# Two PSUM evacuations that may run on ScalarE or VectorE, in an attention and feed-forward kernel whose order a scheduler writes

## The chip, the cores and the metric

The kernel runs on one core of a Trainium2 chip. The metric is the device time of one execution, in microseconds, as the median of several runs. A profiled execution gives the trace from which the rows below are read. Engines are named as in the profile: PE is the matrix engine (PEld its weight loads), ACT is ScalarE, DVE is VectorE, POOL is GpSimd, SP issues most of the DMAs (SPq in the trace).

## The reference, cut to what matters

```python
# S = 2048 rows, D = 448, H = 16 heads of 28, N = 4 segments of 512 rows, F = 1792
g = sigmoid((x * gate_w).sum(-1, keepdims=True))
for s in range(4):                                   # a: attention with a memory
    p = softmax(qs @ ks.T * scale + mask)            # inside the segment
    o = gb * (phi(qs) @ M / (phi(qs) @ z + 1e-6)) + (1 - gb) * (p @ vs)
    M, z = M + phi(ks).T @ vs, z + phi(ks).sum()
a = concat(o) @ wo
b = silu(x @ w1) @ w2                                # the feed-forward
out = g * a + (1 - g) * b
```

## The kernel before

Matrix operands are split into a high and a low half in 16 bits, and a product is the sum of three products of halves. The program is one stream per engine. Nobody writes that stream by hand: every step is handed to `Sched` as a task with its engine, a cost, the steps it depends on, the buffers it takes and a priority, and `Sched.run` picks the next task of each engine by earliest possible start and then by priority. A task may name two engines; `start_of` then lets an engine have it only if it would not end later there than on the other engine by more than `slack`. The constants at the head of the file (priorities, offsets, prices) are the table that shapes this order.

The stages in the order of time:

- Loads, splitting, and the projections q, k, v for all four segments (up to about 163 us in the trace before). The memory part of the attention runs here too (L1052, L1054, L1089, L1090).
- The change of stage (about 146 to 185 us): the first feed-forward products (L632 on `wa`, the first weight matrix, with the short last pieces of two products at L1238 and L1239), the maxima of the scores for the first heads (PE L737, then DVE L744 to L750) and the first softmax heads all start here.
- The attention of the 64 pairs of head and segment, between which feed-forward products are placed (185 to 458 us). One head is a chain: four score matmuls (PE L1355) into three PSUM tiles `sc`; three exponentials (ACT L1360) into `pf`; two causal masks (POOL L1363, L1366); the high half (ACT L1372); the low half in three pieces (POOL L1376); twenty short matmuls with v (PE L1389); one sum (DVE L1397).
- The second half of the feed-forward and the output product (L632 on `wos`), with the result leaving by DVE L1466 and L1470 (458 us to the end).

A feed-forward unit has the steps of `after` in `unit`: e1 is a tanh from PSUM (ACT L1211), e2 multiplies in PSUM (DVE L1213), e3 writes the high half of g to SBUF (ACT L1215), e4 writes the low half (DVE L1217) and frees the PSUM tile. The products with the second weight matrix (PE L1259) read both halves. In the first of the two feed-forward passes each partial sum of 128 rows leaves PSUM by `part` (ACT L1298) for a scratch tensor in HBM.

PSUM has eight tiles: three `sc` (scores, maxima, later the output product), one `cc` for the short attention matmuls, and four (`mm` and a `cc` tile given over at the change of stage) for the feed-forward. Weights pass through two staging tiles `rawf` in turn: SP loads one, ACT L606 writes the high half, DVE L595 or POOL L597 and L598 the low half, and then the staging tile can be loaded again. The rows of q and k of a group of four heads come to SBUF in the tile `ring` by four DMAs, and the maxima of that group (PE L737) wait for all four. SP is one queue: a DMA that waits for a buffer holds back what stands behind it.

Of the kernel before, what the change touches and what calls it, by code (L numbers as in the profile page):

```python
# [13 lines left out]
AF = mybir.ActivationFunctionType  # L14
OP = mybir.AluOpType
# [3 lines left out]
S, D, H, DH, NSEG, L, F = 2048, 448, 16, 28, 4, 512, 1792  # L19
# [8 lines left out]
SCALE = DH ** -0.5  # L28
LIFT = 8.0 * math.log(2.0)
TALL = 2.0 ** 15  # L30
TWINP = 165.57
TWO = 0.33
NEG = -1.0e30
NT = NSEG * NG
# [12 lines left out]
DOWN = 2.0 ** -19  # L47
TINY = 2.0 ** -40
FIT = 2.0 ** -15
WOT = 154.32  # L50
TUS = 1.6
TLAT = 4.0
SLACK = -0.5
LOP = 35.82
LATE = -0.07
FIRST = 165.32
WPRIO = 28.79
MAXO = 63.55
FULL = 0.111
LOCK = 0.06  # L60
RB = "cc"
# [2 lines left out]
VA = 12.33  # L64
VS = 0.91
NV = 8
XH0 = -75.6
NF = 4
VE = 6.18
LASTQ = 6.73  # L70
WQS = -122.17
VH = 29.33
XS0 = -34.76
VC = -7.5
OT1 = -143.04
XS = 35.55
QS = -29.35
KS1 = -24.75
SS = -14.29

# [3 lines left out]


PRICE = 267.48
PRICE2 = 150.04
SLACK2 = 0.15
PVRUNS = [((1, 0), 1)]
PVP = 86.58  # L90
FLO = 41.44
FHI = 709.77
WOP = 85.61
SZ = 13.48
SZSTEP = 0.12
XPRIO = 324.18
WBP = 27.13
XLEAD = 146.82


# [180 lines left out]
def infini_mix(ctx: ExitStack, tc: tile.TileContext, x, wq, wk, wv, wo, beta, w1, w2, out):  # L281
    nc = tc.nc
    out = out.rearrange("b s d -> (b s) d")
    ctx.enter_context(tc.manual_schedule())
    sch = Sched()
# [47 lines left out]
    def act(cols, fn, *deps, **k):  # L333
        return sch.add("ACT", 0.06 + 0.00083 * cols, fn, deps, **k)
# [13 lines left out]
    def either(cols, fn, *deps, **k):  # L348
        eng = {"DVE": nc.vector, "POOL": nc.gpsimd}
        return sch.add(("DVE", "POOL"), (0.07 + 0.00104 * cols, 0.1 + 0.00224 * cols), lambda e: fn(eng[e]), deps, port=True, **k)  # L350

    def scaled(cols, fn, *deps, **k):
        eng = {"DVE": nc.vector, "POOL": nc.gpsimd}
# [27 lines left out]
    cols, at = {}, 0  # L381
# [17 lines left out]
    ogs = const.tile([128, NSEG * TB], F32, name="ogs")  # L399
# [787 lines left out]
    BK["cc"].give(BK["mm"])  # L1187
    sch.price, sch.slack = PRICE2, SLACK2

# [16 lines left out]
    def unit(s, fs, prio, finish, gate=(), tail=False):  # L1206
        gt = {}
        t1, t2 = {}, {}
        def after(f, ps, g, m, p0):
            th = Buf(TH)  # L1210
            e1 = sact(L, lambda ps=ps, th=th: nc.scalar.activation(th.v, ps.v, AF.Tanh, scale=ths[:, s:s + 1]), m, takes=[th],  # L1211
                     uses=[ps], prio=p0)
            e2 = dve(L, lambda ps=ps, th=th: nc.vector.scalar_tensor_tensor(  # L1213
                ps.v, th.v, 1.0, ps.v, op0=OP.add, op1=OP.mult), e1, uses=[ps, th], prio=p0)
            e3 = act(L, lambda ps=ps, g=g: nc.scalar.activation(g.v[:, 0], ps.v, AF.Copy, scale=DOWN), e2,  # L1215
                     uses=[ps, g], prio=p0)
            e4 = dve(L, lambda ps=ps, g=g: nc.vector.scalar_tensor_tensor(  # L1217
                g.v[:, 1], ps.v, DOWN, g.v[:, 0], op0=OP.mult, op1=OP.subtract), e3, uses=[ps, g], prio=p0)
            gt[f] = g, [e3, e4]
            t1[f] = m  # L1220

        own = [f for f in fs if f != FREE]
        for a, b in zip(own[::2], own[1::2] + [None]):
            held = []
            for f in (a, b):
                if f is None:
                    continue
                p0 = prio(11 * L if b is None else 10.5 * L)
                ps, g = Buf(BK["mm"]), Buf(GTR)
                w, wd = WA[f]  # L1230
# [4 lines left out]
            if b is not None:  # L1235
                def both(held=held):
# [4 lines left out]
                       prio=held[1][4])  # L1241
# [5 lines left out]
        for tb in range(TB):  # L1247
            ps = Buf(BK["mm"])
            p0 = prio(3 * len(fs) * D)
            sl = slice(tb * 128, (tb + 1) * 128)  # L1250
            last, lasts = None, []
            halves = [(0, 3 * D // 4), (3 * D // 4, D)] if tail and tb == TB - 1 else [(0, D)]
            for lo, hi in halves:
                for j, f in enumerate(fs):
                    g, w = gt[f][0], WB[f][0]

                    def go(g=g, w=w, j=j, ps=ps, sl=sl, lo=lo, hi=hi):
                        for i, (y, z) in enumerate(((0, 0), (0, 1), (1, 0))):
# [3 lines left out]
                              takes=[ps] if last is None else [],  # L1262
                              uses=[ps, g, w], prio=p0)
# [31 lines left out]
    def part(s, tb, ps, lasts, prio):  # L1295
        k = s * TB + tb
        a = Buf(PA)
        w = act(D + 110, lambda: nc.scalar.activation(a.v, ps.v[:, :D], AF.Copy, scale=ogs[:, k:k + 1]),  # L1298
                lasts[-1][0], takes=[a], uses=[ps], prio=prio)
        PST[k] = dma(229e3, lambda: start(pscr[s][tb * 128:(tb + 1) * 128, :], a.v), w, uses=[a], prio=prio)  # L1300

    def weights(fs, t1, t2, prio):
# [115 lines left out]
    prio = spread(FLO, FHI, NSEG * len(PASSES[0]) * (11 * L + TB * 3 * D))  # L1418
# [126 lines left out]
```

## Time and profile before

| | |
|---|---|
| median of 3 runs | 550.6 us (549.58 to 551.15) |
| the profiled execution | 550.8 us |
| its span, first to last instruction | 549.0 us |
| mean granted clock of PE | 0.997 |
| PE busy | 538.8 us, 98% of the span |
| DVE, ACT, POOL busy | 74%, 74%, 64% |

The execution is 1.8 us longer than its span. Busy time of PE is the time covered by records of matmuls; a record is longer than the time at which the next one may follow, so short gaps do not show as idle time.

### The profile page before, as it was taken

What the parts mean: (1) busy time and instruction counts of PE and PEld (TensorE: products, weight loads), DVE (VectorE), ACT (ScalarE), POOL (GpSimd) and SP (SyncE); (2) the same over time, 40 slices, a digit from 0 to 9 for tenths busy, and PEclk for the clock granted to TensorE, in tenths of its full rate; (3) what the DMA queues carried; (4) which work ended last, traced back from release to release, by engine and by line L of the source; (5) the groups of instructions that cost most, each with busy time, mean ns of one, the idle gap of its engine ahead of it and who ended that gap; (6) DMA issues with size and microseconds to landing.
All of it is one profiled execution on the core that took longest, in us unless ns stands there. A gap on an engine that the chain in (4) does not pass through costs nothing.

```text
span 549.0 us, 11601 instructions
## 1 busy us (share of the span) xinstructions
PE 538.8 (98%) x4028; PEld 295.7 (54%) x4028; DVE 408.9 (74%) x1005; ACT 406.3 (74%) x696; POOL 354.0 (64%) x552
## 2 busy tenths in 40 slices
PE   9999999999998999999999999999999999999997
PEld 3445656565543565555656555565555554555544
DVE  5999899999758785688756789767897219764473
ACT  5979988765357988799887999789997897601140
POOL 3135476834506779889899989998998997211220
PEclk9999999999998999999999999999999999999999
DMA  8778876635475334233333334454311211789962
GB/s 299 251 235 271 239 231 179 207 97 142 145 194 156 102 87 137 72 84 84 90 86 103 87 89 123 119 154 128 83 38 54 87 51 43 265 210 243 258 167 79
DMA packets 78378, 79.19 MB, mean 144 GB/s; under 512 B 44232, under 2 KB 68040, under 8 KB 78320
## 3 DMA queue, kind: packets, MB, share of 16 engines
q1 hardware_dynamic: 77744, 77.47, 48.9%
q10 hardware_dynamic: 576, 0.99, 0.6%
q8 instruction: 31, 0.51, 0.4%
q14 instruction: 27, 0.22, 0.1%
HBM read 48.41 MB, written 26.09 MB: 136 GB/s over the span
## 4 chain that ended last, share of the span: by engine, by line
PE 72%; ACT 8%; DMA 6%; DVE 6%; POOL 4%; issue 2%; SPq 1%; DVEq 0%; POOLq 0%; ACTq 0%
PE mm L632 18%; PE mm L1259 17%; PE sc L632 10%; PE cc L1259 6%; PE sc L737 5%; PE sc L1355 5%; PE cc L1389 5%; PE cc L632 3%; ACT pf L1360 3%; DMA rawf<-in_w_dram 2%; POOL phl L1376 2%; ACT phl L1372 1%; DMA k_scr<-stg 1%; DMA xraw<-in_x_dram 1%; PE cc L1089 1%
## 5 line engine op out<-in xcount | busy, mean ns | idle before, releaser
L1376 POOL TENSOR_TENSOR phl<-pf,phl 128x384 f16<-128x384 f32 (+1 forms) x192 | 189.5, 1004 | 24.2 <-ACT phl L1372 24.0
L1360 ACT ACTIVATE pf<-sc,lift,es 128x512 f32<-128x512 f32 (+1 forms) x192 | 127.0, 707 | 18.1 <-PE sc L1355 13.4
L750 DVE CUSTOM_DVE_ANT_0 sc<-sc,mk 128x384 f32<-128x384 f32 (+1 forms) x192 | 104.7, 575 | 26.9 <-PE sc L737 25.0
L1259 PE MATMUL mm<-wb,ghl 128*128 128x448 f16 (+2 forms) x516 | 111.9, 348 | 0.1
L632 PE MATMUL mm<-xh,wa 128*128 128x512 f16 x393 | 101.4, 379 | 0.0
L1259 PEld LDWEIGHTS <-ghl 128*128 128x128 f16 x684 | 64.0, 97 | 52.8 <-issue 1.0
L1372 ACT ACTIVATE phl<-pf 128x1280 f16<-128x1280 f32 x64 | 81.3, 1270 | 9.8 <-POOL pf L1366 9.3
L632 PEld LDWEIGHTS <-wa 128*128 128x128 f16 x524 | 49.1, 98 | 51.7 <-issue 5.2
L1355 PE MATMUL sc<-ring 86*128 86x512 f16 (+3 forms) x256 | 63.6, 301 | 1.4 <-DVE mx L750 1.0
L737 PE MATMUL sc<-ring 84*128 84x128 f16 (+3 forms) x256 | 57.2, 300 | 1.6 <-DVE mx L745 0.7
L1389 PEld LDWEIGHTS <-phl 128*128 128x128 f16 x1280 | 41.9, 96 | 9.1 <-issue 0.6
L1397 DVE TENSOR_REDUCE oraw<-cc 128x116 f32<-128x232 f32 x64 | 25.3, 396 | 27.7 <-PE cc L1389 27.1
L643 POOL TENSOR_TENSOR ol<-ol,ml 128x448 f32<-128x448 f32 x12 | 13.6, 1132 | 49.7 <-DMA ol<-o_scr 39.2
L1389 PE MATMUL cc<-vg,phl 128*128 128x29 f16 (+1 forms) x1280 | 43.8, 182 | 0.3 <-POOL phl L1376 0.2
L632 PE MATMUL mm<-xh,wqs 128*128 128x512 f16 x176 | 43.4, 379 | 0.2 <-DVE vt L1022 0.2
L632 PE MATMUL mm<-xh,wks 128*128 128x512 f16 x176 | 42.1, 380 | 0.0
L649 ACT ACTIVATE oh<-ol,os 128x448 f16<-128x448 f32 x16 | 10.6, 664 | 41.3 <-POOL ol L643 41.2
L1259 PE MATMUL cc<-wb,ghl 128*128 128x448 f16 x168 | 38.7, 352 | 0.0
L1355 PEld LDWEIGHTS <-ring 86*128 86x128 f16 x256 | 24.0, 98 | 24.5 <-issue 4.5
L632 PE MATMUL cc<-xh,wa 128*128 128x512 f16 x131 | 34.9, 390 | 0.9 <-DVE ghl L1217 0.9
L632 PE MATMUL sc<-wos,oT 128*128 128x448 f16 x176 | 35.4, 352 | 0.0
L1366 POOL TENSOR_SCALAR_AFFINE_SELECT pf<-pf 128x384 f32<-128x384 f32 x64 | 33.6, 526 | 2.2 <-ACT pf L1360 1.7
(197 smaller groups left out, 958.1 us busy)
## 6 DMA issues: line engine op xcount, KB each, us to landing
rawf<-in_w_dram SPq DMA_DIRECT2D x26, 256.0 KB
rawf<-in_w_dram SPq DMA_DIRECT2D x28, 224.0 KB
v_scr<-vt SPq DMA_DIRECT2D x16, 232.0 KB
vg<-v_scr SPq DMA_DIRECT2D x16, 232.0 KB
xraw<-in_x_dram SPq DMA_DIRECT2D x14, 256.0 KB
q_scr<-stg SPq DMA_DIRECT2D x16, 224.0 KB
ring<-q_scr SPq DMA_DIRECT2D x16, 224.0 KB
k_scr<-stg SPq DMA_DIRECT2D x16, 224.0 KB
```

The costliest lines, as they stand in the source:

```text
L632: nc.tensor.matmul(ps(), *p[i], start=(i == 0), stop=(i == n - 1 and not more))
L643: d = pool(530, lambda: nc.gpsimd.tensor_add(b.v, b.v, m.v), d, e, uses=[b, m], **k)
L737: nc.tensor.matmul(ps.v[:, u:u + n], rg.v[:KS, 0, hh, i * 128:(i + 1) * 128], rg.v[:KS, 1, hh, :n], start=i + t > 0, stop=(i + t > 0 or j ...
L750: nc.vector.tensor_tensor_reduce(r, r, MK[:, L - n:], 1.0, NEG, OP.add, OP.max, mx.v[:, hh, i:i + 1])
L1259: nc.tensor.matmul(ps.v[:, lo:hi], g.v[:, y, sl], w.v[:, z, lo:hi], start=(j == 0 and i == 0), stop=(j == len(fs) - 1 and i == 2))
L1355: nc.tensor.matmul(ps.v[:, e:e + w], rg.v[:KK, 1, hh, j * 128:(j + 1) * 128], rg.v[:KK, 0, hh, j * 128:], start=True, stop=True)
L1360: ex.append(sact(e, lambda b=b, ps=ps, pf=pf, e=e: nc.scalar.activation(pf.v[:, b, :e], ps.v[:, :e], AF.Exp, bias=lift, scale=es[:, s:s + ...
L1366: mk.append(pool(204, lambda pf=pf: nc.gpsimd.affine_select(pf.v[:, :, :128], pf.v[:, :, :128], [[0, 3], [1, 128]], OP.is_ge, 0.0, base=0, ...
L1372: hi = copy(1280, lambda hl=hl, flat=flat: nc.scalar.activation(hl.v[:, 0], flat(), AF.Copy), *mk, takes=[hl], uses=[pf], prio=p0 + 2)
L1376: low = pool(w - u + 22, lambda hl=hl, flat=flat, u=u, w=w: nc.gpsimd.tensor_sub(hl.v[:, 1, u:w], flat()[:, u:w], hl.v[:, 0, u:w]), low, u ...
L1389: nc.tensor.matmul(p[:, i, :2 - z], hl.v[:, z, u:u + 128], vg.v[:, j, hh, :2 - z], start=(z == zs[0] and i == 0), stop=(z == zs[-1] and j ...
L1397: nc.vector.tensor_reduce(orw.v[:, hh], p, axis=AX.X, op=OP.add)
```

## The change

`out_of` is a new helper: a copy out of PSUM with a scale, as a task that names ACT and DVE. Step e3 of a feed-forward unit and the copy in `part` use it in place of `act`; `Sched` thus gives each of these 68 copies to the engine that it thinks ends it first. Sixteen constants of the table have other values, so the order is written anew.

```diff
+    def out_of(cols, fn, *deps, **k):
+        how = {"ACT": lambda o, i, s: nc.scalar.activation(o, i, AF.Copy, scale=s),
+               "DVE": lambda o, i, s: nc.vector.tensor_scalar(o, i, s, None, op0=OP.mult)}
+        return sch.add(("ACT", "DVE"), (0.06 + 0.00083 * cols, 0.07 + 0.00104 * cols), lambda e: fn(how[e]), deps, **k)
...
-            e3 = act(L, lambda ps=ps, g=g: nc.scalar.activation(g.v[:, 0], ps.v, AF.Copy, scale=DOWN), e2,
-                     uses=[ps, g], prio=p0)
+            e3 = out_of(L, lambda e, ps=ps, g=g: e(g.v[:, 0], ps.v, DOWN), e2, uses=[ps, g], prio=p0)
...
-        w = act(D + 110, lambda: nc.scalar.activation(a.v, ps.v[:, :D], AF.Copy, scale=ogs[:, k:k + 1]),
-                lasts[-1][0], takes=[a], uses=[ps], prio=prio)
+        w = out_of(D + 110, lambda e: e(a.v, ps.v[:, :D], ogs[:, k:k + 1]), lasts[-1][0], takes=[a], uses=[ps], prio=prio)
...
-WOT = 154.32
+WOT = 103.91
...
-LATE = -0.07
+LATE = -0.17
...
-SLACK2 = 0.15
+SLACK2 = -0.35
```

In the program as built, 15 of the 52 copies of g's high half and 6 of the 16 partial sums stand on DVE (L354 of the changed kernel), the others on ACT (L353). The number of PE instructions of each kind is the same. Up to the first maxima of scores (about 106 us in the trace before) PE's rows are the same, and after that they differ in place only. In the changed kernel line numbers from L351 on are 3 to 5 higher: L1217 is L1221 there, L750 is L755, L1215 is L353, L595 is L600, L606 is L611, L1360 is L1363 and L1372 is L1375.

Three places show how rows moved, all at the change of stage.

On DVE, around the low half (L1217) of the third pair of units, whose PSUM tiles are `cc_2216` and an `mm` tile; `L750` pairs are maxima of scores, `wb` is a piece of the second weight matrix. Before, and then now:

```order
L750 ISA sc_2358,mx<-sc_2358,mk 128x512
L750 ISA mx 128x1
L750 ISA sc_2365,mx<-sc_2365,mk 128x384
L750 ISA mx 128x1
L595 SCALAR_TENSOR_TENSOR wb<-rawf,up,wb 128x448
L1217 SCALAR_TENSOR_TENSOR ghl<-cc_2216,ghl 128x512
L1217 SCALAR_TENSOR_TENSOR ghl<-mm_2243,ghl 128x512
```

```order
L755 ISA sc_2359,mx<-sc_2359,mk 128x512
L755 ISA mx 128x1
L1221 SCALAR_TENSOR_TENSOR ghl<-cc_2216,ghl 128x512
L755 ISA sc_2367,mx<-sc_2367,mk 128x384
L755 ISA mx 128x1
L600 SCALAR_TENSOR_TENSOR wb<-rawf,up,wb 128x448 x2
L1221 SCALAR_TENSOR_TENSOR ghl<-mm_2244,ghl 128x512
```

The low half that frees the `cc` tile now stands ahead of one pair of maxima and of the weight piece; the one that frees the `mm` tile now stands behind two weight pieces instead of one.

On SP, the loads of the third `ring` tile (`ring_2133`), between loads of the staging tiles. Before, and then now:

```order
L366 DMA rawf<-in_w_dram 128x448
L366 DMA ring_2133<-q_scr 56x2048
L366 DMA rawf<-in_w_dram 128x448
L366 DMA vg<-v_scr 128x4x232
L366 DMA ring_2133<-q_scr 28x2048
L366 DMA ring_2133<-k_scr 56x2048
L366 DMA rawf<-in_w_dram 128x448
L366 DMA ring_2133<-k_scr 28x2048
```

```order
L371 DMA rawf<-in_w_dram 128x448 x2
L371 DMA ring_2133<-q_scr 56x2048
L371 DMA vg<-v_scr 128x4x232
L371 DMA ring_2133<-q_scr 28x2048
L371 DMA ring_2133<-k_scr 56x2048
L371 DMA rawf<-in_w_dram 128x448 x2
L371 DMA ring_2133<-k_scr 28x2048
```

The last of the four loads of the ring tile now stands behind two staging loads where it stood behind one; each of the two waits for its own staging tile.

On ACT, around the first exponentials and the high half of the first head (`phl`). Before, and then now:

```order
L1360 ACTIVATE pf<-sc_2342,lift,es 128x512
L1360 ACTIVATE pf<-sc_2346,lift,es 128x256
L606 ACTIVATE wb<-rawf,up 128x448
L1215 ACTIVATE ghl<-cc_2216 128x512
L1215 ACTIVATE ghl<-mm_2243 128x512
L1372 ACTIVATE phl<-pf 128x1280
```

```order
L1363 ACTIVATE pf<-sc_2342,lift,es 128x512
L611 ACTIVATE wb<-rawf,up 128x448
L1363 ACTIVATE pf<-sc_2352,lift,es 128x256
L353 ACTIVATE ghl<-cc_2216 128x512
L353 ACTIVATE ghl<-mm_2244 128x512
L611 ACTIVATE wb<-rawf,up 128x448
L1375 ACTIVATE phl<-pf 128x1280
```

A second weight piece now stands between the two high halves of g and the high half of the first head; these two copies of g stay on ACT.

More of the change, by code (lines that the diff above doesn't have):

```diff
@@ L30 @@
 TALL = 2.0 ** 15
-TWINP = 165.57
+TWINP = 125.24
 TWO = 0.33
@@ L53 @@
 SLACK = -0.5
-LOP = 35.82
-LATE = -0.07
-FIRST = 165.32
+LOP = 26.69
+LATE = -0.17
+FIRST = 167.33
 WPRIO = 28.79
-MAXO = 63.55
+MAXO = 63.47
 FULL = 0.111
@@ L66 @@
 NV = 8
-XH0 = -75.6
+XH0 = -75.5
 NF = 4
@@ L70 @@
 LASTQ = 6.73
-WQS = -122.17
+WQS = -125.76
 VH = 29.33
@@ L76 @@
 XS = 35.55
-QS = -29.35
+QS = -29.51
 KS1 = -24.75
@@ L86 @@
 PRICE = 267.48
-PRICE2 = 150.04
-SLACK2 = 0.15
+PRICE2 = 110.34
+SLACK2 = -0.35
 PVRUNS = [((1, 0), 1)]
[L90 to L93, printed above, removed]
+PVP = 91.33
+FLO = 47.63
+FHI = 707.54
+WOP = 80.08
 SZ = 13.48
@@ L96 @@
 XPRIO = 324.18
-WBP = 27.13
+WBP = 30.46
 XLEAD = 146.82
```

## The prediction

> **What bounds the kernel now.** I read the head of the page first.
>
> ```profile
> span 549.0 us, 11601 instructions
> PE 538.8 (98%) x4028; PEld 295.7 (54%) x4028; DVE 408.9 (74%) x1005; ACT 406.3 (74%) x696; POOL 354.0 (64%) x552
> ```
>
> PE's records cover all of the span but 10.2 us, and the change takes no matmul away. So only PE's gaps can be won or made longer. The second view is busy time by stretch: the front, whose PE order is the same; the rest of the projections; the change of stage and two stretches in it; the attention and its two worst stretches; the output stage; the end.
>
> ```profile
> core 0: us, PE busy (x) PEld busy (x) DVE busy (x) ACT busy (x) POOL busy (x), PEclk, DMA share, GB/s
> 0.00:107.00 107.00, 104.66 (x555) 57.31 (x556) 95.68 (x221) 89.72 (x212) 53.64 (x132) 1.00 0.77 240
> 107.00:163.00 56.00, 56.00 (x323) 31.36 (x321) 44.67 (x97) 29.13 (x58) 19.82 (x42) 1.00 0.50 145
> 163.00:185.00 22.00, 19.22 (x122) 8.87 (x121) 17.92 (x51) 18.55 (x30) 15.16 (x18) 0.92 0.48 127
> 171.50:174.90 3.40, 1.84 (x9) 0.75 (x9) 2.79 (x8) 3.40 (x6) 1.39 (x2) 1.00 0.93 253
> 174.90:178.30 3.40, 3.40 (x12) 1.37 (x12) 3.27 (x7) 3.40 (x6) 2.24 (x4) 0.51 0.18 58
> 185.00:458.00 273.00, 271.55 (x2546) 153.54 (x2545) 196.19 (x545) 242.56 (x357) 245.79 (x344) 1.00 0.33 93
> 249.00:260.00 11.00, 10.32 (x110) 5.82 (x109) 8.99 (x26) 10.72 (x18) 10.58 (x16) 1.00 0.35 87
> 395.00:416.00 21.00, 20.41 (x198) 11.41 (x197) 17.83 (x49) 19.99 (x33) 18.40 (x27) 1.00 0.18 48
> 458.00:544.00 86.00, 86.00 (x477) 43.58 (x474) 53.59 (x93) 26.34 (x43) 19.60 (x19) 1.00 0.72 197
> 544.00:549.00 5.00, 1.40 (x18) 1.02 (x16) 0.81 (x2) 0.00 (x0) 0.00 (x0) 1.00 0.15 46
> ```
>
> Length minus PE busy gives the gaps: 2.34 us in the front, none to 163, 2.78 at the change of stage, 1.45 in the attention (0.68 and 0.59 of it in the two stretches), none in the output stage, 3.60 at the end. The front and the end are not touched. What lies open is 2.78 + 1.45 = 4.2 us, and one thing more: from 174.9 to 178.3 us the granted clock is 0.51, which costs 3.40 x 0.49 = 1.7 us. All that a better order could win is thus about 5.9 us, 1.1%. PE's timeline shows the same stretch:
>
> ```profile
> 173.41 0.81 PE L632 MATMUL cc<-xh,wa 128*128 128x512 f16 x3 [0.87 <-DVE ghl L1217]
> 174.82 0.51 PE L737 MATMUL sc<-ring 84*128 84x128 f16 x4 [0.29 <-DMA ring<-k_scr]
> 175.65 2.77 PE L632 MATMUL cc<-xh,wa 128*128 128x512 f16 x6
> 180.11 1.46 PE L632 MATMUL mm<-xh,wa 128*128 128x512 f16 x6
> ```
>
> Six products of 512 columns take 2.77 us here and 1.46 us five microseconds later. The cause stands in the window just ahead: PE was busy for only 1.84 of 3.40 us and lost half its clock for as long again. [...]
>
> The waits of PE name who ended them:
>
> ```profile
> PE sc L1355 <- DVE mx L750: 1.0, 3, 0.5
> PE cc L632 <- DVE ghl L1217: 0.9, 1, 0.9
> PE sc L737 <- DMA ring<-k_scr: 0.3, 1, 0.3
> PE sc L737 <- ACT pf L1360: 0.3, 1, 0.3
> ```
>
> They are waits for PSUM tiles that DVE or ACT have not emptied yet, and one for a DMA.
>
> **The engines' work.** What the moved copies cost on each side is read from groups of the same shape or nearest to it.
>
> ```profile
> L1215 ACT ACTIVATE ghl<-mm 128x512 f16<-128x512 f32 x39 | 22.3, 597 | 3.2 <-DVE mm L1213 3.1
> L1298 ACT ACTIVATE pa<-mm,ogs 128x448 f32<-128x448 f32 x12 | 7.5, 628 | 0.6 <-PE mm L1259 0.6
> L960 DVE TENSOR_SCALAR pp<-mm,tqk 112x512 f32<-112x512 f32 x6 | 4.3, 728 | 0.0
> L1217 DVE SCALAR_TENSOR_TENSOR ghl<-mm,ghl 128x512 f16<-128x512 f32 x39 | 26.3, 683 | 0.5 <-ACT ghl L1215 0.3
> L1470 DVE SCALAR_TENSOR_TENSOR y<-mm,ogs,ya 128x448 f32<-128x448 f32 x11 | 7.5, 683 | 1.3 <-PE mm L1259 1.0
> ```
>
> ACT loses 15 x 0.597 + 6 x 0.628 = 12.7 us. DVE has no row of a copy to 16 bits out of PSUM: 0.683 and 0.728 bound it, and I take 0.70, between them; for 448 columns I take L1470's 0.683 as it is. That makes 15 x 0.70 + 6 x 0.683 = 14.6 us on DVE. In the attention ACT stands at 242.56 of 273 us (89%), DVE at 196.19 (72%), POOL at 245.79 (90%). If all of it fell there, ACT would go to 84% and DVE to 77%. POOL stays at 90% and paces the heads as before, so ACT's relief can shorten waits but not the stage.
>
> Each copy is dearer on DVE by 0.06 to 0.13 us, 2.3 us at most in sum (15 x 0.131 + 6 x 0.055), and hidden as long as PE has other products to run, which the windows say it has nearly always. [...] Were every copy on the path, the forecast would be higher by those 2.3 us.
>
> **The change of stage, by hand.** These are the rows of DVE, ACT and SP around PE's wait.
>
> ```profile
> 171.56 0.60 DVE L750 CUSTOM_DVE_ANT_0 sc<-sc,mk 128x384 f32<-128x384 f32 x1
> 172.08 0.68 DVE L595 SCALAR_TENSOR_TENSOR wb<-rawf,up,wb 128x448 f16<-128x448 f32 x1
> 172.67 0.68 DVE L1217 SCALAR_TENSOR_TENSOR ghl<-cc,ghl 128x512 f16<-128x512 f32 x1
> ...
> 171.19 0.59 ACT L1215 ACTIVATE ghl<-cc 128x512 f16<-128x512 f32 x1
> 172.15 1.28 ACT L1372 ACTIVATE phl<-pf 128x1280 f16<-128x1280 f32 x1
> ...
> 169.80 0.36 SPq L366 DMA_DIRECT2D rawf<-in_w_dram  x1
> 171.41 0.38 SPq L366 DMA_DIRECT2D ring<-k_scr  x1
> 172.78 0.36 SPq L366 DMA_DIRECT2D rawf<-in_w_dram  x1
> 173.18 0.41 SPq L366 DMA_DIRECT2D ring<-k_scr  x1
> ```
>
> *The freed tile.* PE's 0.87 us wait at 173.41 is for L1217, which started at 172.67 though its input left ACT at 171.78: the maxima and the weight piece stood ahead. Both now stand behind it, so it starts about 0.6 us earlier. Gain 0.0 to 0.87; I take 0.6. What is late next is the maxima pair behind it, 0.68 us later; the score tile that it frees is wanted only after six more products.
>
> *The ring tile.* PE's four matmuls at 174.82 wait for the load that SP issued at 173.18, so it takes 1.6 us to land. Now two staging loads stand ahead of it. The second one waits for the low half of a weight piece on DVE, which waits for its high half on ACT, behind the two copies of g (before, the row after these started at 172.15). Worked on: high half to about 173.0, the low halves of both pieces on DVE to about 174.3, the staging load 0.4, the ring load at about 174.7, landed at 176.3. PE reaches these matmuls later as well, since ten products now come between L1217's tile and them where three did: 172.8 + 10 x 0.24 (1.46 / 6) and two score matmuls of together 0.3, about 175.5. So PE waits 0.8 us where it waited 0.29. Cost 0 to 1.5; I take 0.5. Queued behind the ring load is only the small store of row maxima, which left at 180.92 before.
>
> *ACT's queue.* The second weight piece puts the high half of the first head back by about 0.6 us, and all heads' chains with it. The first head's twenty matmuls are also placed later in PE's row (all ten products of the second unit of that pair come ahead of them, where three did). I take 0, bounds -0.3 and +0.7.
>
> *The half clock.* It comes or it doesn't: 0 or -1.7. PE's share in the 3.4 us ahead of it would be larger, with six products in one piece from about 172.9, but the new wait at 175.6 may hand the next stretch the same fate. I take 0.
>
> Sum of the stage: -0.6 + 0.5 + 0 + 0 = -0.1, between -2.9 and +2.2.
>
> **The attention.** Of its 1.45 us of gaps the two stretches hold 1.27. ACT is busy for 10.72 of 11.00 and 19.99 of 21.00 us there, so it is at the bound just where PE waits, and 12.7 us less on it over the stage should take half of that: -0.6. Bounds: -1.45 (all gaps go), and +1.5 (a fresh order has as many gaps again elsewhere, from DVE's maxima, which already hold PE for 1.0 us).
>
> **The rest.** From 107 to 163 us PE has no gap; the retrieval and memory products are permuted there. I take 0, bounds 0 and +0.5. The output stage has no gap with ACT at 26.34 and POOL at 19.60 of 86 us; 0.
>
> **Sum.** 550.8 (the profiled execution: 549.0 of span and 1.8 around it) - 0.1 - 0.6 = 550.1 us. That execution is 0.2 us over the median of 550.6, so the median should be 549.9 us.
>
> **Rivals.**
>
> *The order gives nothing back.* PE is full, the moved copies were hidden, and gaps only change place: 550.6 us. The change does what it says (21 copies stand on DVE), but nothing waits for it. For it: 98% and 86.00 of 86.00. It lies inside the band of no change, with the forecast.
>
> *The ring load holds PE and the half clock stays (slower).* Place: the third ring tile. It decides as soon as the load is issued after about 175.7, that is, when the second weight piece leaves DVE 1 us later than I worked out; its staging load and ACT's queue are both able to do that. PE then waits 1.5 us more than before, a second stretch of 3.4 us falls to half clock (1.7 us), and the heads behind start late with ACT full (18.55 of 22.00 us in the stage), so nothing is won in the attention: 549.9 + 0.6 + 1.5 + 1.7 = 553.7, say 553.5 us. For it: the SP rows; four loads of a ring tile, and the last one is the one that PE waited for already. Against: the wait was only 0.29 us.
>
> *The half clock does not come and ACT's gaps go (faster).* 550.6 - 1.7 - 1.3 = 547.6 us. For it: the tile that PE waited for longest is freed earlier, and ACT is relieved where it is full. Against: POOL at 90% is untouched. [...]
>
> **Chances.** A measurement of this kernel tells about 0.3% from no change, 1.65 us: under 548.95 is faster, over 552.25 slower. The forecast with the empty order 0.42; faster case 0.26; slower case 0.32, the heavier side because the old order has no gap at all in 56 and in 86 us (107 to 163, 458 to 544) where the new one may open some. The range reaches to both cases: 547.3 to 553.8 us. The likeliest case by itself spans 549.0 to 552.2.
>
> **What would show it.** Right: 21 copies on DVE of 0.65 to 0.73 us each; PE's gaps from 185 to 458 us under 1.45 us; L1217's wait at the change of stage under 0.5 us; a wait of PE for `ring<-k_scr` between 0.3 and 1.5 us. Wrong: two stretches of half clock, or none; PE's gaps in the attention over 3 us, with DVE's maxima or ACT's exponentials as their end; any gap of PE from 458 to 544 us.

## The result: 551.9 us, 0.4% slower, and the profile after

The changed kernel takes 551.91 us (median of 15 runs, 549.91 to 553.16), the kernel before 549.6 in the 15 runs beside it: ratio 1.0036, 95% interval 1.0026 to 1.0045. The forecast was 549.9 against 550.6, 0.1% faster. One execution of a later experiment (the kernel before with the copies on DVE) took 3133.8 us, where its eleven others took 549.1 to 550.0; the ratios leave it out. The profiled execution of the changed kernel took 552.32 us. The head of its page and its busy time by stretch (columns as before):

```profile
span 550.6 us, 11594 instructions
PE 540.3 (98%) x4028; PEld 296.4 (54%) x4028; DVE 424.4 (77%) x1031; ACT 397.7 (72%) x675; POOL 348.9 (63%) x543
```

```profile
0.00:107.00 107.00, 104.42 (x544) 56.69 (x545) 94.61 (x218) 88.67 (x208) 52.15 (x128) 1.00 0.79 238
107.00:163.00 56.00, 56.00 (x328) 31.76 (x326) 45.73 (x100) 30.64 (x60) 21.92 (x46) 1.00 0.50 148
163.00:185.00 22.00, 20.57 (x141) 10.10 (x140) 20.37 (x55) 18.33 (x29) 15.59 (x18) 1.00 0.48 130
185.00:458.00 273.00, 270.78 (x2538) 153.22 (x2537) 204.49 (x563) 235.70 (x341) 241.41 (x337) 0.99 0.33 92
249.00:260.00 11.00, 11.00 (x98) 6.15 (x97) 10.20 (x27) 9.97 (x16) 10.60 (x15) 1.00 0.35 97
329.00:334.00 5.00, 3.58 (x36) 1.66 (x35) 4.87 (x16) 4.66 (x8) 4.63 (x6) 1.00 0.73 196
334.30:337.70 3.40, 3.40 (x32) 2.17 (x31) 2.00 (x5) 2.93 (x5) 3.03 (x6) 0.50 0.27 90
458.00:544.00 86.00, 85.57 (x458) 42.65 (x456) 57.74 (x97) 24.36 (x39) 17.84 (x17) 1.00 0.75 199
```

PE has no half clock at the change of stage any more (1.00 from 163 to 185 us), and fewer gaps there (1.43 us where it had 2.78). It has a new half clock at 334.3 us, and just ahead of it a new place with 1.42 us of gaps in 5 us; the old place from 249 to 260 us has no gap now. And the front, whose rows are the same, holds 11 matmuls less in its 107 us (544 where it had 555).

To compare stages I take the start of a matmul minus the work that stands ahead of it in PE's row. Each matmul counts with the commonest distance from its start to the next one's in the trace before (0.215 us for 512 columns in 16 bits, where a record lasts 0.38; two short products that start 3 to 4 ns apart, as at L1238 and L1239, count as one). That difference grows where PE waits or runs at half clock. After minus before, in the two profiled executions:

| up to | lost (+) or won (-), us |
|---|---|
| matmul 540, before the first scores (105 us) | +1.37 |
| the first product of the first head with v (179 us) | -3.51 |
| the same of head 33 | +0.60 |
| the same of head 36 (331 to 340 us) | +2.94 |
| the last matmul | +0.16 |
| sum | +1.56 |

The spans differ by 1.5 us (550.59 and 549.05). So in this pair the new order wins at the change of stage, loses as much in the attention, most of it at one place, and the front, whose rows are the same, makes the difference.

One pair is not the rule. The same sum over the other profiles (their kernels are described below) gives 4.4 to 5.0 us lost at the change of stage in five others with the order of before there, where this one loses 5.7, and 2.2 to 2.4 in all nine with the changed order. The win there is thus 2.0 to 3.5 us. At the place (heads 33 to 36) the order of before loses 0.9 us in each of six profiles; the changed order loses 3.8 in the three profiles with a half clock there, and 2.3 in the three without.

**The change of stage.** PE's, DVE's and SP's rows in the timeline after:

```profile
171.88 0.32 PE L742 MATMUL sc<-ring 84*128 84x384 f16 x1 [0.64 <-ACT pf L1363]
173.10 1.46 PE L637 MATMUL cc<-xh,wa 128*128 128x512 f16 x6 [0.43 <-DVE ghl L1221]
175.91 0.38 PE L742 MATMUL sc<-ring 84*128 84x128 f16 x4
...
172.35 0.69 DVE L1221 SCALAR_TENSOR_TENSOR ghl<-cc,ghl 128x512 f16<-128x512 f32 x1
...
174.19 0.91 SPq L371 DMA_DIRECT2D rawf<-in_w_dram  x2
175.14 0.42 SPq L371 DMA_DIRECT2D ring<-k_scr  x1
```

The low half that frees the `cc` tile waits for nothing but its copy, and PE's wait for it is 0.43 us instead of 0.87. The longest wait is another now: 0.64 us for an exponential, which stands behind a weight piece in ACT's new order. The ring load leaves at 175.14, 2 us later than before, and no row of PE waits for it.

**The place at 331 us.** PE, ACT and DVE in the timeline after:

```profile
330.67 0.60 PE L1358 MATMUL sc<-ring 86*128 86x512 f16 x3
331.68 0.27 PE L1358 MATMUL sc<-ring 86*128 86x256 f16 x1 [0.41 <-DVE mx L755]
332.53 0.32 PE L742 MATMUL sc<-ring 84*128 84x384 f16 x1 [0.58 <-ACT pf L1363]
333.20 0.84 PE L1358 MATMUL sc<-ring 86*128 86x512 f16 x3 [0.35 <-ACT pf L1363]
333.87 2.05 PE L1263 MATMUL mm<-wb,ghl 128*128 128x448 f16 x6
...
330.55 0.69 ACT L1216 ACTIVATE th<-cc,ths 128x512 f32<-128x512 f32 x1 [0.28 <-PE mm L1243]
331.13 0.68 ACT L1216 ACTIVATE th<-mm,ths 128x512 f32<-128x512 f32 x1
331.70 3.42 ACT L1363 ACTIVATE pf<-sc,lift,es 128x512 f32<-128x512 f32 x5
...
331.49 1.14 DVE L454 TENSOR_REDUCE sizes<-rawf 128x1 f32<-128x448 f32 x2
332.54 0.68 DVE L1221 SCALAR_TENSOR_TENSOR ghl<-mm,ghl 128x512 f16<-128x512 f32 x1
```

From 330.4 to 333.8 us PE has only score products to run, and each needs a score tile that the exponentials or the maxima must empty first. On ACT two tanh stand ahead of the five exponentials, the first of them waiting for PE. Six products then take 2.05 us, most of it at half clock. Before, three exponentials stood ahead of the two tanh, and PE had hardly a gap:

```profile
329.00:334.00 5.00, 4.92 (x44) 2.36 (x42) 4.59 (x13) 5.00 (x9) 4.62 (x8) 1.00 0.41 106
...
331.84 1.92 ACT L1360 ACTIVATE pf<-sc,lift,es 128x512 f32<-128x512 f32 x3
333.63 0.71 ACT L1211 ACTIVATE th<-cc,ths 128x512 f32<-128x512 f32 x1
```

**The copies.** The new line on DVE, by shape (count, then min, median and max in ns):

```profile
L354 DVE TENSOR_SCALAR ghl<-mm x10: 678/691/692, 178.9 to 529.1; 128x512 f16<-128x512 f32 x10
L354 DVE TENSOR_SCALAR pa<-mm,ogs x5: 683/683/685, 215.0 to 444.5; 128x448 f32<-128x448 f32 x5
L354 DVE TENSOR_SCALAR ghl<-cc x5: 680/683/692, 252.2 to 472.2; 128x512 f16<-128x512 f32 x5
```

With the one that is not shown (a partial sum out of the `cc` tile, 677 ns) they are 21. They last 0.68 to 0.69 us, where 0.70 and 0.683 were forecast, and no wait is put down to them.

### The profile page after: what moved, and what is told of

It is laid out like the page before. It is cut to its first block, busy times and chain, and to the rows that moved or that the text cites. A ratio compares the mean times of both kernels' runs of the same rounds, so it can differ in the third digit from the quotient of the medians.

```text
span 550.6 us, 11594 instructions
## 1 busy us (share of the span) xinstructions
PE 540.3 (98%) x4028; PEld 296.4 (54%) x4028; DVE 424.4 (77%) x1031; ACT 397.7 (72%) x675; POOL 348.9 (63%) x543
## 4 chain that ended last, share of the span: by engine, by line
PE 74%; ACT 10%; DMA 8%; DVE 4%; issue 2%; POOL 1%; SPq 0%; ACTq 0%; DVEq 0%; POOLq 0%
PE mm L637 20%; PE mm L1263 15%; PE sc L637 9%; PE sc L742 6%; PE cc L1263 5%; PE sc L1358 5%; PE cc L1392 5%; ACT pf L1363 4%; PE cc L637 3%; DMA rawf<-in_w_dram 2%; DMA k_scr<-stg 1%; ACT phl L1375 1%; PE cc L1094 1%; DMA raw<-in_wv_dram 1%; DMA rwo<-in_wo_dram 1%
## 5 line engine op out<-in xcount | busy, mean ns | idle before, releaser
L1363 ACT ACTIVATE pf<-sc,lift,es 128x512 f32<-128x512 f32 (+1 forms) x192 | 126.8, 705 | 18.7 <-PE sc L1358 14.0
L755 DVE CUSTOM_DVE_ANT_0 sc<-sc,mk 128x384 f32<-128x384 f32 (+1 forms) x192 | 104.8, 573 | 21.4 <-PE sc L742 19.7
L1263 PE MATMUL mm<-wb,ghl 128*128 128x448 f16 (+2 forms) x516 | 113.3, 349 | 0.0
L1263 PEld LDWEIGHTS <-ghl 128*128 128x128 f16 x684 | 64.3, 98 | 54.0 <-issue 1.9
L1375 ACT ACTIVATE phl<-pf 128x1280 f16<-128x1280 f32 x64 | 81.2, 1268 | 14.7 <-POOL pf L1369 13.8
L742 PE MATMUL sc<-ring 84*128 84x128 f16 (+3 forms) x256 | 58.8, 302 | 2.1 <-ACT pf L1363 1.5
L1263 PE MATMUL cc<-wb,ghl 128*128 128x448 f16 x168 | 38.8, 352 | 0.0
```

The costliest lines, as they stand in the source:

```text
L742: nc.tensor.matmul(ps.v[:, u:u + n], rg.v[:KS, 0, hh, i * 128:(i + 1) * 128], rg.v[:KS, 1, hh, :n], start=i + t > 0, stop=(i + t > 0 or j ...
L755: nc.vector.tensor_tensor_reduce(r, r, MK[:, L - n:], 1.0, NEG, OP.add, OP.max, mx.v[:, hh, i:i + 1])
L1263: nc.tensor.matmul(ps.v[:, lo:hi], g.v[:, y, sl], w.v[:, z, lo:hi], start=(j == 0 and i == 0), stop=(j == len(fs) - 1 and i == 2))
L1363: ex.append(sact(e, lambda b=b, ps=ps, pf=pf, e=e: nc.scalar.activation(pf.v[:, b, :e], ps.v[:, :e], AF.Exp, bias=lift, scale=es[:, s:s + ...
L1375: hi = copy(1280, lambda hl=hl, flat=flat: nc.scalar.activation(hl.v[:, 0], flat(), AF.Copy), *mk, takes=[hl], uses=[pf], prio=p0 + 2)
```

## The experiments

Theory 1: single places of the order decide, through PE's waits and the half clock after them. Theory 2: the copies on DVE hold back its other work. The front became a question of its own. Kernels of an experiment have their own line numbers; the operation names show what stands there.

**The kernel before once more.** No edit.

> The kernel before, unchanged, to learn how often its own stretch of half clock comes. The 15 runs before fall in two groups, 548.8 to 549.7 us (nine) and 550.0 to 551.4 us (six); the profiled one, 550.8 us with a mean clock of 0.997, had a half clock from 174.9 to 178.3 us, which costs 1.7 us. Both theories expect a median of 549.6 +/- 0.3 us, ratio 1.000 +/- 0.001. The first theory (the time moves by where PE starves and whether the half clock follows) expects the runs at 0.999 near 549.3 us and the runs at 0.997 or below near 550.7 us, about two in five of them.

549.45 us, ratio 1.0004 (0.9994 to 1.0014). The half clock came at 173.6 us. But it is not a matter of two runs in five: in all the 109 runs of the kernel before in these sessions, 101 have a clock under 0.999. Those have a mean of 549.5 us and the other 8 of 549.4, so here the half clock cannot be shown to cost its 1.7 us. In the changed kernel it can: of its 21 runs (the 15 above and six of a later experiment) 13 have it by their mean clock, with a mean of 552.28 us, and the other 8 have a mean of 550.67.

**After's order, copies on ACT; before's order, copies on DVE.** Every engine's order stays, only the engine of the 21 copies is another:

```diff
-                t.fn(t.eng)                                 # after
+                t.fn("ACT" if t.copy else t.eng)
...
-            e3 = act(L, lambda ps=ps, g=g: nc.scalar.activation(g.v[:, 0], ps.v, AF.Copy, scale=DOWN), e2,   # before
+            e3 = act(L, lambda ps=ps, g=g: leave(g.v[:, 0], ps.v, DOWN, (s, f) in MOVED), e2,
```

> The changed kernel with its order on every engine kept, but the 21 copies that stand on VectorE (DVE) issued on ScalarE (ACT) at the same place of the program. Theory 1, the order: the engine of the copies is not the price; the pair of tanh ahead of five exponentials at 331 us stays, so PE still waits there: 551.9 us, +/- 0.5. Theory 2, the copies: 14.3 us of copies on DVE hold back its maxima and low halves, and PE waits for those; with them on ACT the loss goes: 549.6 us, +/- 0.5. If ACT was really relieved by the change, the time rises instead, by up to 1 us over 551.9.

> The kernel before with its order kept, but the same 21 copies (15 of g's high half, 6 partial sums) issued on DVE at the same place of the program. Theory 1, the order: 549.6 us, +/- 0.5: each copy is 0.1 us dearer on DVE and hidden. Theory 2, the copies: 551.5 us or more, with PE waiting for DVE's maxima or low halves over 1 us longer in sum than before.

The first takes 557.53 us (ratio 1.0159, 1.0138 to 1.0179), 5.6 more than the change with its copies on DVE. Its waits:

```profile
PE sc L744 <- ACT pf L1365: 2.5, 6, 0.6
PE sc L1360 <- ACT pf L1365: 1.7, 4, 0.6
PE cc L639 <- DVE ghl L1223: 1.2, 2, 0.7
PE mm L639 <- DVE ghl L1223: 1.1, 1, 1.1
```

PE waits 4.2 us for exponentials, where the profile after has 1.8 (1.5 and 0.3), and 2.3 us for low halves, where it has 0.7. In the order that was made for them, the copies on DVE are worth 5.6 us; the last sentence of the expectation had the direction and at most 1 us of it. The second takes 549.68 us (1.0001, 0.9992 to 1.0010): in the order of before they are worth nothing and cost nothing. Theory 2 falls with both.

**The helper alone, the table alone.** Edits: the changed kernel with the old table but `FIRST = 167.33`; the kernel before with the new table but `WBP = 27.13`.

> The helper alone: the changed kernel with the table of before, but for one constant (FIRST 167.33, as in the changed kernel: with the whole old table the scheduler finds no order that closes). It puts 34 of the 68 copies on DVE and writes a third order. Theory 1, the order at single places: the time follows from this order's own gaps, to be read from its trace: 549.0 to 553.0 us, no relation to the number of copies on DVE. Theory 2, the copies: 34 copies on DVE cost more than 21 do: 553 us or more. On the front (all rows the same up to 105 us): in the three profiles with the order of before, matmul number 540 of PE starts at 104.5 to 105.0 us, in the three with the changed order at 105.6 to 106.4. If that is chance, here it may lie anywhere from 104.5 to 106.4.

> The table alone: the kernel before with the table of the changed kernel, but for one constant (WBP 27.13, as before: with the whole new table and no choice of engine the scheduler finds no order that closes). All 68 copies stay on ACT. Theory 1, the order at single places: again an order of its own, 549.0 to 553.0 us by its gaps; if the new table carries both the gain at the change of stage and the place at 331 us, 551 to 552 us. Theory 2, the copies: with none on DVE 549.6 us, +/- 0.5. On the front: as the changed kernel (matmul 540 at 105.6 to 106.4 us) if it goes with the table, as before if it goes with the helper, anywhere between if it is chance.

564.27 us (1.0264, 1.0234 to 1.0293) and 554.55 us (1.0084, 1.0065 to 1.0104): each alone is worse than both together, and both lie outside the 549 to 553 us of theory 1. The first, with 34 copies on DVE, is where theory 2 put it, so by itself it does not speak against that theory; the second has no copy on DVE and is slow all the same. Their orders have half clocks of their own, in all 17.1 us long in the first and 6.8 in the second. What a table is worth can't be split from the helper that it was drawn for.

**The place at 331 us, mended and made.** On ACT, in the changed kernel the first edit, in the kernel before the reverse:

```diff
-ACTIVATE th<-cc,ths 128x512
-ACTIVATE th<-mm,ths 128x512
 ACTIVATE pf<-sc,lift,es 128x512 x2
 ACTIVATE pf<-sc,lift,es 128x256
+ACTIVATE th<-cc,ths 128x512
+ACTIVATE th<-mm,ths 128x512
```

> The changed kernel with one place of ACT's order changed: at 330.5 us the two tanh of a feed-forward pair stand behind the three exponentials of the head, as in the kernel before, instead of ahead of them. All else is the same. Theory 1, the place: the exponentials start about 0.6 us earlier, PE's waits of 0.58 and 0.35 us at 332.5 and 333.2 us go, PE is busy enough that the half clock from 334.3 us (1.7 us) does not come: 0.9 + 1.7 x 2/3 (the share of the runs of the changed kernel with a clock of 0.997 or below) = 2.0 us less, 549.9 us, +/- 0.5. Theory 2, the copies: DVE's copies are where they were, so 551.5 us or more.

550.91 us (1.0030, 1.0016 to 1.0045). The median is 1.0 less than that of the change, where 2.0 was expected, but the intervals of the two ratios overlap, so the gain in time is not shown. The clock is 0.999 or more in 11 of 12 runs: the half clock went. PE's rows show that the gaps did not:

```profile
331.08 0.27 PE L1369 MATMUL sc<-ring 86*128 86x256 f16 x1 [0.41 <-DVE mx L766]
331.98 0.83 PE L1369 MATMUL sc<-ring 86*128 86x512 f16 x3 [0.35 <-ACT pf L1374]
334.26 0.38 PE L753 MATMUL sc<-ring 84*128 84x512 f16 x1 [0.18 <-ACT pf L1374]
334.93 0.38 PE L753 MATMUL sc<-ring 84*128 84x128 f16 x4 [0.29 <-ACT pf L1374]
```

They are spread over 4 us now, since the next head's exponentials stand behind the tanh.

> The kernel before with one place of ACT's order changed, as the changed kernel has it: at 331.8 us the two tanh of a feed-forward pair stand ahead of the three exponentials of the head instead of behind them. No copy is on DVE. The tanh can't start before 333.2 us (PE ends their products then), so the exponentials end about 2.5 us later than now. Theory 1, the place: PE finds no free score tile, waits 1.5 to 2.5 us there, and a half clock of 3.4 us (1.7 us) follows: 549.5 + 2.0 + 1.7 = 553.2 us, +/- 1. If the feed-forward products that stand behind fill the wait: 549.5 to 550.5. Theory 2, the copies: 549.6 us, since no copy moves.

553.92 us (1.0084, 1.0061 to 1.0107): one swap among five rows of ACT costs 4.6 us. PE's rows, and the busy time in the 3.41 us before and during the half clock:

```profile
334.52 0.32 PE L757 MATMUL sc<-ring 84*128 84x384 f16 x1 [2.02 <-ACT pf L1380]
335.19 0.94 PE L757 MATMUL sc<-ring 84*128 84x512 f16 x2 [0.35 <-ACT pf L1380]
```

```profile
331.79:335.20 3.41, 1.04 (x9) 0.30 (x5) 1.17 (x3) 2.67 (x5) 0.80 (x1) 1.00 0.58 167
335.20:338.61 3.41, 3.41 (x10) 1.29 (x10) 3.10 (x10) 2.44 (x3) 3.24 (x5) 0.50 0.52 150
```

2.4 us of waits and 1.7 of half clock: theory 1 holds, and no copy is on DVE here.

**The place mended on three engines.** Besides ACT's rows as above, on DVE a low half ahead of a pair of maxima and two reductions, on PE twice three products of L1263 ahead of score matmuls.

> The changed kernel with the place at 331 us mended on three engines: the two tanh behind the three exponentials on ACT (as in the run that did this alone), the low half that frees an mm tile ahead of the maxima and of two reductions of weights on DVE, and with that two groups of three products with the second weight matrix moved into PE's row ahead of score matmuls that wait. Theory 1, the place: PE's gaps from 329 to 336 us fall from 1.5 us (with ACT's order alone mended) to 0.5 us, no half clock follows, and the attention and the rest lose 1.3 us to before in place of 3.6; median 550.2 us +/- 0.5 with a slow front, 548.8 with a fast one. Rival: the gaps move behind the place, and it stays at 550.9 us.

552.30 us (1.0046, 1.0031 to 1.0062): the rival was right that the gaps move, though the time is 1.4 us over its 550.9. Six of the eight runs have a half clock by their mean clock (0.997 or less); the profiled one, 550.1 us, has none. In it the gaps have moved 2 us on, most of them into one:

```profile
334.15 0.38 PE L760 MATMUL sc<-ring 84*128 84x512 f16 x1 [1.07 <-ACT pf L1381]
```

The products that were moved forward are missing there, while the exponential that PE waits for still stands behind the two tanh.

**The freed tile alone.** In the kernel before, at the change of stage:

```diff
-SCALAR_TENSOR_TENSOR wb<-rawf,up,wb 128x448          # DVE, L595
 SCALAR_TENSOR_TENSOR ghl<-cc,ghl 128x512             # DVE, L1217
+SCALAR_TENSOR_TENSOR wb<-rawf,up,wb 128x448
...
-DMA rawf<-in_w_dram 128x448                          # SP
 DMA ring<-k_scr 28x2048
+DMA rawf<-in_w_dram 128x448
```

> The kernel before with two rows changed at the change of stage: on DVE the low half that frees the cc tile (L1217 at 172.67 us) ahead of the weight piece (L595), and on SP the last load of the ring tile (173.18 us) ahead of the staging load that stands before it. Theory 1: the half clock from 173.6 to 177.0 us follows from PE's waits just before it, 0.87 us for the low half above all. The low half starts 0.6 us earlier, the ring load 0.4 us earlier, PE is busy for 2.7 instead of 1.84 of the 3.4 us, and the half clock (1.7 us) goes: 549.5 - 0.8 - 1.7 = 547.0 us, +/- 0.5. Rival: the half clock comes from something else at the change of stage and stays: 548.7 us, +/- 0.5, or the delayed weight piece holds PE later: 549.5.

550.03 us (1.0011, 0.9998 to 1.0025). PE's rows:

```profile
171.95 0.81 PE L652 MATMUL cc<-xh,wa 128*128 128x512 f16 x3 [0.28 <-DVE ghl L1237]
173.28 0.38 PE L757 MATMUL sc<-ring 84*128 84x512 f16 x1 [0.53 <-ACT pf L1380]
173.95 0.40 PE L757 MATMUL sc<-ring 84*128 84x128 f16 x4 [0.29 <-ACT pf L1380]
174.79 2.77 PE L652 MATMUL cc<-xh,wa 128*128 128x512 f16 x6
```

The wait fell from 0.87 to 0.28 us as expected, but waits for exponentials of 0.53 and 0.29 us follow, and PE is busy for 2.08 of the 3.40 us from 170.8, where 2.7 was expected. The half clock stayed, as the rival had it, and the time is no better than the 549.5 of the rival's second half.

**The front.** Up to 105 us both programs hold the same instructions in the same order with the same waits, yet the rows of the first loads differ. From 3 to 5 us (the last number is GB/s), and the last row common to both, in the kernel before (its second profile) and in the changed one:

```profile
3.00:5.00 2.00, 2.00 (x6) 0.60 (x4) 0.00 (x0) 1.14 (x2) 1.70 (x10) 1.00 0.98 355
...
105.00 0.38 PE L733 MATMUL sc<-maskb,identb 128*128 128x512 bf16 x1
```

```profile
3.00:5.00 2.00, 2.00 (x6) 0.61 (x4) 0.00 (x0) 1.14 (x2) 1.70 (x11) 1.00 0.93 197
...
106.89 0.38 PE L738 MATMUL sc<-maskb,identb 128*128 128x512 bf16 x1
```

> The changed kernel, unchanged, for the front and for the half clock. Read so far: up to 105 us both kernels hold the same instructions, yet in five profiles of kernels with the order of before matmul 540 of PE starts at 104.5 to 105.0 us, in five with a redrawn order at 105.6 to 106.4; from 4 to 5 us the first loads move at 362 to 374 GB/s in the former and 228 to 249 GB/s in the latter. Theory F1, it goes with the program: here again 228 to 249 GB/s and 105.6 us or more, median 551.9 us +/- 0.6. Theory F2, it goes with where a run's buffers come to lie, by chance: as likely 362 to 374 GB/s and under 105.1 us, and then the median falls by 1.2 us or more, to 550.5. On the half clock: all stretches seen begin a whole multiple of 3.413 us after the first full clock, so it should here too.

551.37 us (1.0033, 1.0018 to 1.0048), 227 GB/s, matmul 540 at 105.71: it goes with the program. Then streams were made longer or shorter where it changes no result:

```diff
     sch.run()                                          # the end of the program
+    spare_ps = BK["mm"].take(Buf(BK["mm"]))
+    for _ in range(2):                                  # 20 in the kernel before
+        nc.tensor.matmul(spare_ps[:, :8], maskb, maskb[:, :8], start=True, stop=True)
+    for _ in range(5):                                  # not in the kernel before
+        nc.gpsimd.memset(gate[:, :1], 0.0)
...
-WARM = 8                                               # the kernel before, made shorter
+WARM = 6
```

> The changed kernel with two matmuls of 8 columns and five one-column memsets on POOL behind the last output step, which change no result: the instruction streams of PE and POOL get as long as in the kernel before (7,891 and 690 instructions instead of 7,887 and 685; before has 7,890 and 690). All else is the same. If the slow first loads come from the length of these two streams (by where the program's parts then lie in memory), the first loads move at 362 to 374 GB/s from 4 to 5 us, matmul 540 starts under 105.1 us, and the median falls by 1.2 us or more. If not: 228 to 249 GB/s, 105.6 us or more, 551.9 us +/- 0.6.

> The kernel before with twenty matmuls of 8 columns behind its last matmul (40 more instructions for PE), which change no result and run while the last output is on its way. If the length of the program's streams decides on the speed of the first loads, they may fall to 228 to 249 GB/s from 4 to 5 us, with matmul 540 at 105.6 us or more and 1.2 us or more on the median (550.7 us); if the order decides: 362 to 374 GB/s, under 105.1 us, 549.5 us +/- 0.4.

> The changed kernel with the two spare matmuls behind its last one alone (PE's stream 7,891 instructions instead of 7,887, POOL's as it was). If the length of PE's stream decides, the first loads move at 350 GB/s or more from 4 to 5 us, matmul 540 starts under 105.1 us, and the median is 549.2 us +/- 0.5, as with both streams longer. If POOL's decides: 228 to 249 GB/s, 105.4 us or more, 551.4 us +/- 0.6.

> The changed kernel with the five memsets on POOL alone (690 instructions instead of 685, PE's as it was, 7,887). If POOL's stream decides: 350 GB/s or more, 549.2 us +/- 0.5. If PE's decides: 228 to 249 GB/s, 551.4 us +/- 0.6.

> The kernel before with six instead of eight dummy matmuls at its start (7,886 instructions on PE instead of 7,890; they feed nothing, and run while the first loads are on their way). If the length of PE's stream decides, the first loads fall to 228 to 249 GB/s from 4 to 5 us, matmul 540 starts at 105.4 us or later, and the median rises by 1.2 to 2 us, to 551.0 us +/- 0.5. If it doesn't: 350 GB/s or more, 549.4 us +/- 0.5.

Instructions are counted in the program as built, matmuls, weight loads and waits together; the first two are equal in number before and after:

| kernel | instructions for PE | GB/s, 4 to 5 us | matmul 540, us | median, us (ratio to before, interval) |
|---|---|---|---|---|
| after | 7,887 | 228 | 106.38 | 551.91 (1.0036, 1.0026 to 1.0045) |
| after, longer PE and POOL | 7,891 | 359 | 103.93 | 549.20 (0.9999, 0.9986 to 1.0013) |
| after, longer PE | 7,891 | 373 | 104.14 | 550.29 (1.0009, 0.9998 to 1.0020) |
| after, longer POOL | 7,887 | 247 | 105.96 | 551.28 (1.0042, 1.0025 to 1.0059) |
| before | 7,890 | 374 | 105.01 | 549.60 |
| before, longer PE | 7,930 | 356 | 104.85 | 548.98 (0.9990, 0.9981 to 0.9999) |
| before, shorter PE | 7,886 | 229 | 105.95 (the same row, two matmuls less ahead) | 552.20 (1.0055, 1.0039 to 1.0070) |

Four instructions at the end of PE's stream, which run behind its last product, take 1.6 to 2.7 us away (1.1 to 2.2 from the 551.37 of the second measurement). The median with a longer PE alone lies 0.6 us over the expected span: in these two rows too the half clock makes the difference, with a mean of 550.5 us in the ten runs that have it by their mean clock and of 548.9 in the ten others. Two dummy matmuls less make the kernel before slow in the same way. (Six instead of eight also leave PE idler at the start, busy for 1.70 us from 3 to 5 us instead of 2.00, and three of its four runs have a mean clock of 0.992 where before has 0.997, so not all of its 2.85 us need be this.) In the 18 profiles the nine with 7,890 or more all have 356 GB/s or more, the nine with 7,887 or fewer 249 or less. POOL's stream has no part in it: made longer alone, it leaves them at 247. PE's row in the same two stretches, longer PE alone, and before made shorter:

```profile
3.00:5.00 2.00, 2.00 (x6) 0.60 (x4) 0.00 (x0) 1.14 (x2) 1.71 (x10) 1.00 0.97 343
...
104.65 0.38 PE L738 MATMUL sc<-maskb,identb 128*128 128x512 bf16 x1
```

```profile
3.00:5.00 2.00, 1.70 (x6) 0.50 (x4) 0.00 (x0) 1.15 (x2) 1.70 (x10) 1.00 0.93 199
...
106.46 0.38 PE L733 MATMUL sc<-maskb,identb 128*128 128x512 bf16 x1
```

**Both that helped.** The changed kernel with the tanh behind the exponentials and the longer streams.

> The changed kernel with both additions that helped: the two tanh behind the three exponentials at 331 us, and the longer streams of PE and POOL. From the sums of the traces: behind the front it is worth 0.5 to 0.8 us less than before (3.0 us won at the change of stage, 2.2 to 2.5 lost later, no half clock), and the front is that of before: 548.7 us +/- 0.4, where the kernel before has 549.4 and the changed kernel with longer streams alone 549.2 (with a half clock in four of its ten runs). If the place at 331 us is worth nothing once the front is right: 549.2.

549.04 us (0.9995, 0.9986 to 1.0003), with no half clock in any of 11 runs: 0.3 us under before, which can't be told from it. In its profile (550.15 us, at the upper end of its runs) the first loads move at 378 GB/s, and matmul 540 comes at 105.28 all the same: fast first loads do not settle the whole front.

## Why the prediction was wrong, step by step

**The first step that failed: "The front and the end are not touched."** Equal rows were taken for equal time, so the front stood in the sum with nothing. The changed program has three instructions less on PE, its first loads (3 to 5 us) run at 197 GB/s where two profiles of before have 334 and 355, and 1.4 us are lost before the first changed row. With the length put right (the two kernels with a longer PE, ten runs each), the change takes 549.7 us, against 549.4 for before over 109 runs.

**The second: relief on ACT takes gaps of the attention away (-0.6).** It came out at about +3.7 in the first pair of profiles. ACT's share fell from 89% to 86%, and the old gaps near 255 us went, but a fresh order opened a new place, the bound of +1.5 that was named for it being too small. The place costs 1.4 us more than before by its gaps alone, and 2.9 with the half clock that follows them in 13 of 21 runs. Two rows of ACT moved ahead in the kernel before were enough to make such a place there; moved back in the changed kernel they took the half clock away, but not the gaps, so the rows around them have a part in it. The bound left out the half clock, which came behind the gaps of this place in 13 of 21 runs and cost 1.6 to 1.7 us there.

**What the two make together** can be read from four means: 552.28 and 550.67 us with and without the half clock, 550.5 and 548.9 with the length of PE's stream put right. The front is worth 1.7 to 1.8 us, the half clock 1.6 to 1.7 us in 13 of 21 runs, so 1.0 on the average. The last mean is 0.6 us under the 549.5 of before. A part of that is again the front: with the longer streams matmul 540 starts at 103.93 and 104.14, where in before it starts at 104.49 and 105.01. That these 0.6 are close to the 0.7 that was forecast is luck, since the parts were far off and cancel, and so is it that 551.91 lies within the span that was given: no rival had the front.

**The change of stage** was forecast at -0.1 and won 2.0 to 3.5 us. *The freed tile* was right in kind: PE's wait for it is 0.44 us shorter, where 0.6 was taken, and L1221 started as soon as its copy was done. *ACT's queue*, taken at 0, made PE wait 0.64 us for an exponential, inside its bound of +0.7 but by another row than the one named. *The half clock* was taken at 0 and went: the emptiest 3.41 us there have PE busy for 2.35 us, against 1.84 of 3.40 before. This was the mechanism of the faster case, but what it is worth stays open, since its price of 1.7 us came from one profile and the 8 runs of before without it are no faster.

*The ring tile* was a misreading, and the expected wait never came. PE's four matmuls at 174.82 did not wait for the load that left at 173.18: by the records of its semaphore, that load was complete at 176.50 us, more than a microsecond after they had started. They start 0.05 us after ACT ended an exponential, and the second profile of before puts the same wait down to it:

```profile
173.49 0.53 PE L737 MATMUL sc<-ring 84*128 84x128 f16 x4 [0.29 <-ACT pf L1360]
```

So the 1.6 us from issue to landing (it was 3.3), the 0.8 us that PE would wait, the 0.5 that was taken and the rival that hung on them had no ground. In the changed kernel the load left at 175.14, where 174.7 was worked out, and was complete at 178.30 without a wait of PE for it.

**The copies** were right: duration, count, and that they are hidden, shown by the order of before with the copies on DVE. What was not foreseen is that in the new order they are needed, 5.6 us' worth.

**The rest** from 107 to 163 us has no gap, as forecast; the output stage has 0.43 us of gaps where none was forecast. Of the signs that were named, the copies' time and the wait for L1217 under 0.5 us came true. PE's gaps from 185 to 458 us (2.22 us, where under 1.45 would have been right) and those of the output stage spoke against the forecast.

## What to carry to other kernels

With PE busy for 98% of the span here, the orders differed behind the front most of all at two places, 2.0 to 3.5 us at the change of stage and 1.4 to 2.9 us at 331 us: look for stretches where PE has only score products, and count a half clock that follows, 1.6 to 1.7 us here, with the gaps. Whoever mends such a place must look at what stands 2 us on, since all three mends tried here moved or spread the wait instead of ending it. And where a whole program is compared for a few tenths of a per cent, compare first a stretch in which nothing was changed: here it held 1.4 of the 1.5 us between the first two profiles, and padding one stream showed that it had nothing to do with the order.

## What the hardware showed that was not expected

*The first loads were faster where PE's stream was longer.* With 7,890 instructions or more (nine profiles) they move at 326 to 355 GB/s from 3 to 5 us, with 7,887 or fewer (the other nine) at 197 to 215. From 3 to 4 us a packet takes 74 to 87 ns on the mean in the former and 131 to 170 in the latter, with the same loads asked for at the same times (within 0.04 us in the first pair). From 3 to 5 us only the queues q1 and q10 have packets in that pair (397 before, 231 after), and the two queues that load instructions have none. Why the length matters, and whether it does so again at other lengths, stays open.

*The half clock came on a grid of 3.413 us.* In the first pair of profiles its stretches inside the program begin 170.667 and 327.680 us after the first full clock, 50 and 96 times 3.4133 us, and each lasts 3.413 us by the records of the clock. All 16 stretches inside the 18 profiles begin a whole multiple of that length (to 0.01 us) after the first full clock, 49 to 138 of them, and last one or two such windows. By PE's records, from 105 to 540 us, every window at full clock with PE busy under 2.3 us of its 3.41 was followed by a stretch (1.87 us ahead of that in the kernel before, 1.99 ahead of that in the changed one); of those from 2.3 to 2.7 us two were and most were not; above 2.7 none. Near the end of the program that did not hold: in windows that begin at 541 to 547 us, nine with PE busy for 1.65 to 2.23 us were followed by none. Nor was PE idle for a whole window ahead of any of the 16: it was busy for 0.8 to 2.7 us. The first full clock comes anywhere from 3.7 to 6.9 us (4.27 and 6.59 in the first pair), so a place like that at 331 us is cut by the windows in another way in each run; that only 13 of 21 runs have the half clock fits this, but no run was made to show it.
